# Dynamic convolution, layer norm and feed-forward: the first softmax in two pieces, the last tiles one by one, and a new order of the work at the start

## The chip, the cores and the metric

The kernel runs on one core of one Trainium2 chip. What counts is the time of one execution on the device in microseconds (us). Five engines work side by side, each through its own list of instructions in order: TensorE (PE; its weight loads are counted apart as PEld), VectorE (DVE), ScalarE (ACT), GpSimd (POOL) and SyncE (SP), which here issues transfers. Sixteen DMA engines carry the transfers.

## What is computed

`x` is (8, 4224, 192) and `weight_gen` (8, 4224, 8, 7), both float32. The reference, with the shapes put in, is:

```python
w = np.exp(w - np.max(w, axis=-1, keepdims=True))        # 8 heads, 7 taps for each token
w = w / (np.sum(w, axis=-1, keepdims=True) + 1e-09)
x_unf = x_pad[:, idx, :].reshape(B, S, 7, 8, 24)         # the token and the six before it
x = np.einsum('bshk,bskhg->bshg', w, x_unf).reshape(B, S, 192)
mu = np.mean(x, axis=-1, keepdims=True)
var = np.mean((x - mu) ** 2, axis=-1, keepdims=True)
xn = (x - mu) / np.sqrt(var + 1e-06) * g_ln
out = x + np.maximum(xn @ w_ch1, 0.0) @ w_ch2            # 192 -> 768 -> 192
```

The three parameters of the second half are float64.

## The kernel before

**Tiles.** The 33,792 tokens lie as 128 partitions by 264 tiles: a partition holds 264 neighbouring tokens, and a tile is one token of each partition, 192 values wide. The tiles go through in `PARTS` of 4, 4, 8 (five times), 12 (seventeen times), 8 and 4 tiles. The convolution works on chunks of 2 tiles (the first part), 4 tiles (the parts of 4 and 8) or 6 tiles (the parts of 12); the feed-forward works on groups of `NT` = 4 tiles. `SOFT` = (4, 8, 12, ...) says how many tiles one softmax covers.

**Softmax** (`softmax`, L449 to 487). After the load of the weights `w` come six steps, each for one softmax: the maximum over the taps (VectorE, L466), `sub` (GpSimd, L468), the exponential (ScalarE, L469), the sum (VectorE, L482), its logarithm (ScalarE, L484) and `less` (GpSimd, L486), which leaves the logarithm of the weights in `e`. A last exponential (`expw`, ScalarE, L498) is made for each chunk and puts its weights into PSUM (`wn`). For the chunks below `PMUL` = 3 there is one more (`keep`, L502), which puts them into `e` for GpSimd.

**Convolution** (`conv`, L492 to 577). A chunk has four multiplications by x, all L535: `c0`, `c1` and `c3` are two taps each and write one of five `pr` buffers, `c2` is one tap and writes `y`. VectorE runs them with the weights in `wn`, except `c3` of the chunks below `PMUL`, which GpSimd runs with the weights in `e`. In the first three chunks TensorE adds the seven products up (L560). In all later ones GpSimd does: two transfers that add one half of a `pr` buffer to the other (`d0`, `d1`, L541) and four additions to `y` (`a0` to `a3`, L538). So VectorE needs a free `pr` buffer for each multiplication of two taps, and GpSimd frees it.

**Norm** (`norm`, L598 on). For parts that begin below tile `STATS` = 8, VectorE takes mean and variance with `bn_stats`, two tiles at a time (L628). For the others ScalarE makes a sum (L611) and a sum of squares (L616) of each tile. Then come the root (ScalarE), a Newton step (VectorE) and the scaled tile `xh` (ScalarE, L686). The first two groups are turned on TensorE (L710), the others split into high and low fp16 halves and turned by a transfer (L756 to 762).

**Feed-forward.** The weights arrive as float64 words; VectorE makes float32 of them (L955, L964), then their power of two (`w_scale`, L982 to 988), from which ScalarE and TensorE make fp16 halves. For each group TensorE makes three `unit` products into `ph` (L780); each is evicted by ScalarE (`relu`, L796) and VectorE (`hlo`, the low half, L798). Two products (`p0`, `p1`, L832) bring the result into `po`, and VectorE merges it into `y` (L884), which is stored (L892). For the last group `output` (L861) does this for two tiles at a time, with one merge and one store for each pair.

**What sets the order.** Every operation has a name and a tile, and the table `PLACE` gives its place in one global order. Each engine runs its own operations in that order, so an operation waits for all that its engine has ahead of it. At the start, SyncE issues the weights of the first softmax (`w`, 4 tiles), those of the second (8 tiles), and then the first chunk's x in three transfers: `h0` (four tiles of the tokens ahead), `h` (the other two and the two tiles of the chunk) and `f` (the chunk's tiles in the partitions that begin a batch). The first multiplication (`c0`) needs `h0` alone, the second (`c1`) needs `h` too. Ahead of all of it ScalarE loads its table (L368) and makes a negated identity (`minus`, L380).

## Time and profile before

| | us |
|---|---|
| median of 3 runs (lowest, highest) | 844.35 (843.34, 845.62) |
| the profiled execution's own time | 843.82 |
| its span in the trace | 842.0 |
| busy: PE, DVE, ACT, POOL | 821.4, 736.5, 683.8, 701.6 |
| mean granted TensorE clock, as a share of full speed | 0.994 |

The span is the time from the first to the last instruction that the trace has; the 1.8 us around it belong to the execution but show no instruction. Busy times are sums over the whole span: TensorE is busy for 98% of it and the others for 81% to 87%. Since the start, the middle and the end of the program have different limits, the shares of the whole say little, and the rows below are read by stretch.

### The profile page before, as it was taken

To read this page: it belongs to the slowest core of one execution; us is meant where nothing else is said; L and a number is where in the kernel's file an instruction comes from. 1 tells how busy PE (TensorE), PEld (TensorE's weight loads), DVE (VectorE), ACT (ScalarE), POOL (GpSimd) and SP (SyncE) were. 2 spreads that over 40 slices of the span, in tenths; PEclk is the share of its full clock that TensorE was granted. 3 is DMA by queue.
4 is the path that set the end of the run, shared out by engine and by line. 5 is a ranking of instruction groups with operands and counts; after the bars stand their busy time and mean duration, and the time that the engine had idled before them with its cause. 6 is when DMAs were issued, how large, how long until landed. Compare 5 with 4: busy or idle time off the path is not lost.

```text
span 842.0 us, 37407 instructions
## 1 busy us (share of the span) xinstructions
PE 821.4 (98%) x16724; PEld 811.3 (96%) x16724; DVE 736.5 (87%) x685; ACT 683.8 (81%) x1774; POOL 701.6 (83%) x402
## 2 busy tenths in 40 slices
PE   6889999999999999999999999999999999999997
PEld 5669999999999999999999999999999999999997
DVE  7999999999999999999999999999989896745332
ACT  3899998898998899898888979988888878776431
POOL 4999999999999999999999999899798879624000
PEclk9889999999999999999999999999999999999999
DMA  9997997989999997889878997777877766352432
GB/s 228 206 211 153 221 162 170 204 160 205 193 195 191 199 215 167 178 186 215 190 153 202 188 217 174 164 185 163 180 153 162 165 145 129 78 116 68 80 65 58
DMA packets 133887, 140.88 MB, mean 167 GB/s; under 512 B 104294, under 2 KB 106222, under 8 KB 133726
## 3 DMA queue, kind: packets, MB, share of 16 engines
q1 hardware_dynamic: 120190, 88.16, 45.9%
q0 software_dynamic: 13536, 50.34, 30.8%
q8 instruction: 130, 2.13, 1.0%
q14 instruction: 31, 0.25, 0.1%
HBM read 36.43 MB, written 25.95 MB: 74 GB/s over the span
## 4 chain that ended last, share of the span: by engine, by line
PE 82%; DVE 11%; issue 2%; POOL 2%; ACT 1%; DMA 1%; SPq 1%; DVEq 0%; POOLq 0%; ACTq 0%
PE po L832 41%; PE ph L780 40%; DVE pr L535 6%; DVE hlo L798 2%; DVE y L535 1%; POOL y L538 1%; DMA x<-in_x_dram 1%; PE ph L861 1%; DVE y L884 1%; POOL pr L541 1%; ACT hh L796 0%; DVE mx L466 0%; ACT junk L611 0%; DVE sm L482 0%; DVE s L628 0%
## 5 line engine op out<-in xcount | busy, mean ns | idle before, releaser
L538 POOL TENSOR_TENSOR y<-y,pr 128x1152 f32<-128x1152 f32 (+1 forms) x188 | 488.3, 2625 | 13.0 <-DVE y L535 4.3
L780 PE MATMUL ph<-xT,c_w 64*128 64x256 f16 x7128 | 412.9, 269 | 1.9 <-DVE hlo L798 1.3
L780 PEld LDWEIGHTS <-c_w 64*128 64x128 f16 x7128 | 386.2, 94 | 3.1 <-issue 2.9
L832 PE MATMUL po<-c_w2h,hh 64*128 64x192 f16 x3120 | 388.0, 243 | 1.1 <-DVE y L884 1.1
L832 PE MATMUL po<-c_w2l,hh 64*128 64x192 f16 x3120 | 388.0, 243 | 0.0
L832 PE MATMUL po<-c_w2h,hlo 64*128 64x192 f16 x3120 | 388.0, 243 | 0.0
L535 DVE TENSOR_TENSOR pr<-x,wn 128x2304 f32<-128x2304 f32 (+2 forms) x147 | 333.2, 2276 | 4.3 <-POOL y L538 2.5
L832 PEld LDWEIGHTS <-hh 64*128 64x128 f16 x6240 | 309.7, 94 | 1.4 <-issue 1.3
L798 DVE SCALAR_TENSOR_TENSOR hlo<-ph,hh 128x1024 f16<-128x1024 f32 x198 | 239.4, 1217 | 73.1 <-ACT hh L796 72.6
L796 ACT ACTIVATE hh<-ph 128x1024 f16<-128x1024 f32 x198 | 200.2, 1014 | 84.8 <-PE ph L780 80.6
L832 PEld LDWEIGHTS <-hlo 64*128 64x128 f16 x3120 | 177.6, 94 | 0.0
L758 POOL TENSOR_TENSOR hl<-xh,hl 128x768 f16<-128x768 f32 x64 | 114.7, 1828 | 49.1 <-ACT hl L756 48.3
L686 ACT ACTIVATE xh<-y,s 128x192 f32<-128x192 f32 x264 | 125.8, 536 | 17.2 <-DVE s L674 12.1
L616 ACT ACTIVATE junk<-y,s 128x192 f32<-128x192 f32 x256 | 115.8, 452 | 7.9 <-PE po L832 1.8
L541 POOL DMA_DIRECT2D pr<-pr x94 | 93.2, 1054 | 26.6 <-DVE pr L535 22.1
L611 ACT ACTIVATE junk<-y 128x192 f32<-128x192 f32 x256 | 92.1, 360 | 12.5 <-PE po L832 4.1
L884 DVE SCALAR_TENSOR_TENSOR y<-po,c_fs,y 128x768 f32<-128x768 f32 (+1 forms) x83 | 67.9, 835 | 7.4 <-PE po L832 7.2
L535 DVE TENSOR_TENSOR y<-x,wn 128x1152 f32<-128x1152 f32 (+2 forms) x50 | 59.9, 1199 | 0.0
L756 ACT ACTIVATE hl<-xh 128x768 f16<-128x768 f32 x64 | 53.4, 836 | 1.6 <-PE po L832 0.7
L611 ACT ACTIVATION_READ_ACCUMULATOR junk<-y 128x1 f32 x256 | 48.1, 188 | 0.0
L616 ACT ACTIVATION_READ_ACCUMULATOR junk<-y,s 128x1 f32 x256 | 47.9, 187 | 0.0
L486 POOL TENSOR_TENSOR e<-e,sm 128x672 f32<-128x672 f32 (+2 forms) x23 | 37.8, 1645 | 6.6 <-ACT sm L484 6.6
(86 smaller groups left out, 308.3 us busy)
## 6 DMA issues: line engine op xcount, KB each, us to landing
pr<-pr POOLq DMA_DIRECT2D x68, 576.0 KB, 6.1
x<-in_x_dram SPq DMA_DIRECT2D x34, 576.0 KB, 6.0
...
pr<-pr POOLq DMA_DIRECT2D x26, 384.0 KB, 5.0
...
x<-in_x_dram SPq DMA_DIRECT2D x14, 384.0 KB, 6.2
out_dram<-y SPq DMA_DIRECT2D x13, 384.0 KB, 5.2
...
```

Source lines behind the costliest of these rows:

```text
L535: E.tensor_tensor(out=ov, in0=xv, in1=wv, op=ALU.mult)
L538: Q.tensor_tensor(out=flat(0), in0=flat(0), in1=flat(k), op=ALU.add)
L541: return Q.dma_start(flat(to), flat(k), accum_op=ALU.add, max_dma_last_dim=CHUNK * D * 4)
L611: A.activation(junk, at(y)[:, j, :], AF.Identity, scale=-SQ / D, accum_out=at(s4)[:, 3, t : t + 1])
L616: A.activation(junk, at(y)[:, j, :], AF.Square, scale=SQ, bias=at(s4)[:, 3, t : t + 1], accum_out=at(s4)[:, 0, t : t + 1])
L686: A.activation(paired(xh, t), at(y)[:, i, :].rearrange("p (c q) -> p c q", q=P // 2), AF.Identity, bias=row(2 if quick else 3)[:, g + t : ...
L758: lambda xh=xh, hl=hl: Q.tensor_tensor(out=halves(hl, True), in0=pairs(xh), in1=halves(hl, False), op=ALU.subtract),
L780: T_.matmul(ph[:, r, v * 2 * P : (v + 1) * 2 * P], W["w1"][rows, WB[r][c], w, f : f + P], xv[rows, a, c, :, :], start=(v == 0 and k == 0), ...
L796: lambda: A.activation(at(hh)[:, us, :], at(ph), AF.Relu), [ph], [(hh, u)])
L798: lambda: V.scalar_tensor_tensor(out=at(hlo)[:, us, :], in0=at(ph), scalar=0.0, in1=at(hh)[:, us, :], op0=ALU.max, op1=ALU.subtract),
L832: made.append(T_.matmul(at(po)[:, z, e * D : (e + 1) * D], token(b, 2 * z + e, j)[rows], W[w][rows, j, :], start=(ph == 0 and e == 0 and k ...
L884: V.scalar_tensor_tensor(out=ysl, in0=at(po)[:, zs[0] : zs[-1] + 1, : 2 * D], scalar=W["fs"][:, 0:1], in1=ysl, op0=ALU.mult, op1=ALU.add)
```

## The change

- The first softmax of 4 tiles becomes two of 2 tiles (`SOFT`), with pools of their own (`w0`, `e0`). One transfer brings the weights of both. In the first piece (`SUBV`, `LESSV`) both subtractions are VectorE's; in the second they stay GpSimd's.
- ScalarE, not SyncE, issues the second transfer of the first x (`h`). Its table load and `minus`, which stood ahead of everything, become operations with places of their own.
- GpSimd gets `c1` of the second chunk (`PTWO`) and `c3` of the fourth (`PMUL` 3 to 4), with the extra copies of the weights (`keep`) that they need.
- `STATS` = (4,) names the parts with `bn_stats`: the first part (tiles 0 to 3) now has ScalarE's sums and squares, the second still has `bn_stats`.
- `last` takes the place of `output`: the last four tiles go one by one, each with its own half of a PSUM buffer and a merge of 192 elements, with stores of two tiles, one and one.
- `PLACE` is a new table up to about place 495; from there on it is the old one, moved by about 11.

The diff, without all but two lines of the table:

```diff
 PARTS = (4,) * 2 + (8,) * 5 + (12,) * 17 + (8, 4)
-SOFT = (4, 8) + (12,) * 21
+SOFT = (2, 2, 8) + (12,) * 21
-PMUL = 3
-STATS = 8
+PMUL = 4
+STATS = (4,)
+PTWO = (2,)
+SUBV = (0,)
+LESSV = (0,)
...
-    'wload': (0, 1, 15, 26, 98, 102, 176, 495, 321, 482, 657, 761, 837, 1034, 613, 1145, 1282, 1182, 951, 1438,
+    'wload': (0, 3, 13, 46, 85, 190, 243, 505, 428, 102, 668, 772, 848, 1045, 624, 1156, 1293, 1193, 962, 1449,
...
+    pool("w0", 1, [P, 2 * FIRST, HK], F32)
+    pool("e0", 2, [P, FIRST * H, K], F32)
...
-    A.preload_act_table_set("natural_log_exp_and_others")
...
-    A.activation(minus, ident, AF.Copy, scale=-1.0)
...
-            sp(want, lambda: first(cut, PAD + n - cut), [], [("x", "h"), *cols], dma_ns((PAD + n - cut) * D * 4), "load")
+            op("ACT", 620, want, lambda: first(cut, PAD + n - cut, A), w=[("x", "h"), *cols],
+               dma=dma_ns((PAD + n - cut) * D * 4), kind="load")
+            op("ACT", 1300, ("table", 0), lambda: A.preload_act_table_set("natural_log_exp_and_others"), w=["table"])
+            op("ACT", 310, ("minus", 0), lambda: A.activation(minus, ident, AF.Copy, scale=-1.0), ["table"], ["minus"])
...
-        wb = pa["w"] = Buf("w")
-        sp(("wload", t0), lambda: SY.dma_start(at(wb)[:, :n, :].rearrange("p t f -> p (t f)"), tokens(wf, t0, n)), [], [wb],
+        if t0 == FIRST:
+            pa["w"] = softs[0]["w"]
+            return
+        wb = pa["w"] = Buf("w" if t0 else "w0")
+        n = n if t0 else 2 * FIRST
+        sp(("wload", t0), lambda: SY.dma_start(at(wb)[:, :n, :].rearrange("p t f -> p (t f)"), tokens(wf, t0, n)), [], [wb] if t0 else [(wb, 0), (wb, FIRST)],
...
-        step("Pool", 100 + 1.82 * m * K, "sub",
-             lambda: Q.tensor_tensor(out=at(e)[:, :m], in0=a3(wb), in1=wide(mx), op=ALU.subtract), [wb, mx], [e])
+        E, name, ns = (V, "V", v_ns(m * K)) if S0 in SUBV else (Q, "Pool", 100 + 1.82 * m * K)
+        step(name, ns, "sub",
+             lambda E=E: E.tensor_tensor(out=at(e)[:, :m], in0=a3(wb), in1=wide(mx), op=ALU.subtract), [wk, mx], [e])
...
-            if c < PMUL and i == 3:
+            if c < PMUL and (i == 3 or i == 1 and t0 in PTWO):
...
-        quick = S0 < STATS
+        quick = S0 in STATS
...
+    def last(gp, t, s):
+        e = t % 2
+        if e == 0:
+            gp["po"] = Buf("ph")
+        po, ks = gp["po"], triples(gp)
+        def mm():
+            for k, (b, j, w) in enumerate(ks):
+                T_.matmul(at(po)[:, e, :D], token(b, t, j), W[w][:, j, :], start=k == 0, stop=k == len(ks) - 1)
+        op("PE", 1490, ("o", s), mm, whole(gp), [(po, e), "pe"], lat=360.0)
+        y, j = ycol(gp["pa"], gp["g"] + t)
+        def final():
+            V.scalar_tensor_tensor(out=at(y)[:, j, :], in0=at(po)[:, e, :D], scalar=W["fs"][:, 0:1],
+                                   in1=at(y)[:, j, :], op0=ALU.mult, op1=ALU.add)
+        op("V", v_ns(D, 63), ("f", s), final, [(po, e), "fs"], [(y, j)])
+        if t > 0:
+            i, n = (j, 1) if t > 1 else (j - 1, 2)
+            t0 = chunks[-1]["S"] + i
+            sp(("u", s), lambda: SY.dma_start(tokens(out, t0, n), at(y)[:, i : i + n, :].rearrange("p t d -> p (t d)")),
+               [(y, i + q) for q in range(n)], [], dma_ns(n * D * 2))
...
     for t in range(NT):
-        output(prev, t, C)
+        last(prev, t, C)
```

The table moves instructions on every engine; three places show it. In the rows below a name's last number is the program's own count, and the number before it is the buffer.

First, VectorE at the start, before: maxima and sums of the first and second softmax (L466, L482), and the first multiplications (L535).

```order
L466 TENSOR_REDUCE mx0_92<-w0_64 128x32
L482 TENSOR_REDUCE sm0_94<-w0_64 128x32
L466 TENSOR_REDUCE mx1_93<-w1_65 128x64
L535 TENSOR_TENSOR pr0_76<-x_63,wn0_102 128x2x384
L535 TENSOR_TENSOR y0_67<-x_63,wn0_102 128x384
L482 TENSOR_REDUCE sm1_95<-w1_65 128x64
L535 TENSOR_TENSOR pr1_77<-x_63,wn0_102 128x2x384
L535 TENSOR_TENSOR pr2_78<-x_63,wn1_103 128x2x384
L535 TENSOR_TENSOR pr4_80<-x_63,wn1_103 128x2x384
```

The same place in the changed kernel (L481 maximum, L484 `sub`, L498 sum, L503 `less`, L552 multiplication; `w00` is the pair of pieces, `e01` the first piece):

```order
L481 TENSOR_REDUCE mx0_95<-w00_67 128x16
L481 TENSOR_REDUCE mx1_96<-w00_67 128x16
L484 TENSOR_TENSOR e01_69<-w00_67,mx1_96 128x112
L498 TENSOR_REDUCE sm0_97<-w00_67 128x16
L503 TENSOR_TENSOR e01_69<-e01_69,sm0_97 128x112
L552 TENSOR_TENSOR pr0_79<-x_63,wn0_105 128x2x384
L498 TENSOR_REDUCE sm1_98<-w00_67 128x16
L552 TENSOR_TENSOR y0_70<-x_63,wn0_105 128x384
L481 TENSOR_REDUCE mx0_95<-w0_64 128x64
L552 TENSOR_TENSOR pr1_80<-x_63,wn0_105 128x2x384
L498 TENSOR_REDUCE sm0_97<-w0_64 128x64
```

The first piece now passes through VectorE alone but for ScalarE's steps, the sum of the second piece stands behind the first multiplication, and the maximum and sum of the 8-tile softmax (`w0`) stand two and one multiplications further back than before.

Second, GpSimd at the start, before: the subtractions of the first three softmaxes (L468, L486), its `c3` of the first three chunks (L535) and the first additions by transfer (L541).

```order
L468 TENSOR_TENSOR e0_96<-w0_64,mx0_92 128x224
L486 TENSOR_TENSOR e0_96<-e0_96,sm0_94 128x224
L468 TENSOR_TENSOR e1_97<-w1_65,mx1_93 128x448
L486 TENSOR_TENSOR e1_97<-e1_97,sm1_95 128x448
L535 TENSOR_TENSOR pr3_79<-x_63,e0_96 128x2x384 x2
L468 TENSOR_TENSOR e0_96<-w2_66,mx0_92 128x672
L535 TENSOR_TENSOR pr4_80<-x_63,e1_97 128x2x768
L541 DMA pr3_79<-pr3_79 128x768
L541 DMA pr2_78<-pr2_78 128x768
```

In the changed kernel (L484, L503 subtractions, L552 multiplications, L555 additions, L558 additions by transfer):

```order
L484 TENSOR_TENSOR e00_68<-w00_67,mx0_95 128x112
L503 TENSOR_TENSOR e00_68<-e00_68,sm1_98 128x112
L484 TENSOR_TENSOR e0_99<-w0_64,mx0_95 128x448
L552 TENSOR_TENSOR pr2_81<-x_63,e01_69 128x2x384
L503 TENSOR_TENSOR e0_99<-e0_99,sm0_97 128x448
L552 TENSOR_TENSOR pr4_83<-x_63,e00_68 128x2x384
L552 TENSOR_TENSOR pr1_80<-x_63,e00_68 128x2x384
L484 TENSOR_TENSOR e1_100<-w1_65,mx1_96 128x672
L552 TENSOR_TENSOR pr2_81<-x_63,e0_99 128x2x768
L555 TENSOR_TENSOR y3_73<-y3_73,pr2_81 128x768
L558 DMA pr3_82<-pr3_82 128x768
```

GpSimd has lost the two subtractions of the first piece and has two more multiplications, `pr1_80` (`c1` of the second chunk) and the second `pr2_81` from `e0_99` (`c3` of the fourth); its first additions to `y3` now stand among them.

Third, VectorE at its fifth chunk, before: `c0` (`pr4_80`), the power of two of the first weights (L982 to 988), `c3` (`pr3_79`), `c1` (`pr2_78`), and `bn_stats` of the second part (L628) behind all of it.

```order
L535 TENSOR_TENSOR pr4_80<-x_63,wn0_102 128x2x768
L982 TENSOR_SCALAR c_r1_125<-po0_106 128x1
L983 TENSOR_SCALAR c_r1_125<-c_r1_125 128x1
L985 TENSOR_SCALAR c_r1_125<-c_r1_125 128x1
L986 RECIPROCAL c_r1_125<-c_r1_125 128x1
L988 TENSOR_SCALAR c_gi_122<-c_g_121,c_r1_125 128x1 x2
L535 TENSOR_TENSOR pr3_79<-x_63,wn0_102 128x2x768
L535 TENSOR_TENSOR pr2_78<-x_63,wn0_102 128x2x768
L955 SCALAR_TENSOR_TENSOR po0_106<-pr1_77,po0_106 128x384
L964 SCALAR_TENSOR_TENSOR hlo1_91<-x_63,po0_106 128x384
L628 BN_STATS s42_100<-y2_69 128x6 x2
```

In the changed kernel (L552 multiplications, L1023 to 1029 power of two, L645 `bn_stats`):

```order
L552 TENSOR_TENSOR pr0_79<-x_63,wn1_106 128x2x768
L552 TENSOR_TENSOR y4_74<-x_63,wn1_106 128x768
L1023 TENSOR_SCALAR c_r1_126<-po0_109 128x1
L1024 TENSOR_SCALAR c_r1_126<-c_r1_126 128x1
L1026 TENSOR_SCALAR c_r1_126<-c_r1_126 128x1
L1027 RECIPROCAL c_r1_126<-c_r1_126 128x1
L1029 TENSOR_SCALAR c_gi_123<-c_g_122,c_r1_126 128x1 x2
L552 TENSOR_TENSOR pr2_81<-x_63,wn1_106 128x2x768
L645 BN_STATS s41_102<-y2_72 128x6 x2
L552 TENSOR_TENSOR pr3_82<-x_63,wn1_106 128x2x768
```

`c1` (`pr2_81`) and both `bn_stats` now stand ahead of `c3` (`pr3_82`), which stood right behind the power of two.

## Rows read from the trace of the kernel before

**Rows 1.** Busy time by stretch: window, length, engines (instructions), PEclk, DMA share, GB/s.

```profile
0.00:8.00 8.00, 0.00 (x0) 0.00 (x0) 2.19 (x8) 3.44 (x7) 3.76 (x10) 1.00 0.65 166
8.00:20.00 12.00, 11.60 (x58) 11.50 (x59) 11.97 (x16) 4.03 (x11) 5.48 (x5) 1.00 1.06 267
20.00:52.70 32.70, 27.35 (x108) 18.90 (x107) 31.68 (x50) 28.02 (x78) 31.54 (x22) 0.84 0.93 217
52.70:100.00 47.30, 46.30 (x950) 45.81 (x951) 46.96 (x48) 45.55 (x125) 46.61 (x31) 1.00 0.85 184
100.00:148.60 48.60, 47.22 (x1000) 46.77 (x995) 47.06 (x44) 41.31 (x109) 47.37 (x31) 1.00 0.87 174
148.60:800.00 651.40, 651.38 (x13868) 651.22 (x13869) 582.49 (x511) 551.61 (x1437) 565.24 (x306) 1.00 0.79 168
```

**Rows 2.** Timeline of TensorE: the first product (start, duration, instruction, wait before).

```profile
52.72 4.19 PE L780 MATMUL ph<-xT,c_w 64*128 64x256 f16 x72 [0.58 <-ACT c_w2l L1080]
```

**Rows 3.** Who TensorE waited for, 52.6 to 842 us: total, number, longest.

```profile
PE ph L780 <- DVE hlo L798: 1.3, 3, 0.7
PE po L832 <- DVE y L884: 1.1, 1, 1.1
```

**Rows 4.** Chain of waits, 117 to 150 us: start, time, instruction.

```profile
123.47 1.86 POOL y L538
```

**Rows 5.** Who GpSimd waited for, 0 to 48 us: total, number, longest.

```profile
POOL e L486 <- ACT sm L484: 3.9, 2, 2.6
```

**Rows 6.** Timeline, 0 to 9 us: VectorE, GpSimd and ScalarE.

```profile
3.31 0.39 DVE L466 TENSOR_REDUCE mx<-w 128x32 f32<-128x224 f32 x1 [2.28 <-DMA w<-in_weight_gen_dram]
3.78 0.57 POOL L468 TENSOR_TENSOR e<-w,mx 128x224 f32<-128x224 f32 x1 [1.48 <-DVE mx L466]
6.22 0.97 POOL L468 TENSOR_TENSOR e<-w,mx 128x448 f32<-128x448 f32 x1
6.30 0.27 ACT L498 ACTIVATE wn<-e 128x112 f32<-128x112 f32 x1 [0.75 <-POOL e L486]
7.30 0.95 DVE L535 TENSOR_TENSOR pr<-x,wn 128x768 f32<-128x768 f32 x1 [1.58 <-DMA x<-in_x_dram]
```

**Rows 7.** VectorE's groups by form: busy, mean ns of one, idle before.

```profile
L535 DVE TENSOR_TENSOR pr<-x,wn 128x1536 f32<-128x1536 f32 x41 | 70.9, 1744 | 0.1
L884 DVE SCALAR_TENSOR_TENSOR y<-po,c_fs,y 128x768 f32<-128x768 f32 x47 | 47.4, 1009 | 4.4 <-PE po L832 4.3
L535 DVE TENSOR_TENSOR pr<-x,wn 128x768 f32<-128x768 f32 x4 | 3.6, 947 | 1.6 <-DMA x<-in_x_dram 1.6
L628 DVE BATCH_NORM_STATS2 s<-y 128x6 f32<-128x384 f32 x4 | 2.2, 560 | 0.0
L884 DVE SCALAR_TENSOR_TENSOR y<-ph,c_fs,y 128x384 f32<-128x384 f32 x2 | 1.2, 618 | 4.4 <-PE ph L861 4.4
```

**Rows 8.** DMA issues, 0 to 6 us: KB each, median us from issue to landing.

```profile
x<-in_x_dram SPq DMA_DIRECT2D x2, 360.0 KB, 5.3
```

**Rows 9.** GpSimd's multiplications by form.

```profile
L535 POOL TENSOR_TENSOR pr<-x,e 128x768 f32<-128x768 f32 x2 | 3.1, 1547 | 3.2 <-PE ph L560 3.2
L535 POOL TENSOR_TENSOR pr<-x,e 128x1536 f32<-128x1536 f32 x1 | 2.9, 2904 | 1.2 <-ACT e L502 1.2
```

**Rows 10.** ScalarE's sums and squares, from the costliest groups of the page.

```profile
L616 ACT ACTIVATE junk<-y,s 128x192 f32<-128x192 f32 x256 | 115.8, 452 | 7.9 <-PE po L832 1.8
L611 ACT ACTIVATE junk<-y 128x192 f32<-128x192 f32 x256 | 92.1, 360 | 12.5 <-PE po L832 4.1
```

**Rows 11.** Timeline, 20 to 40 us: VectorE and GpSimd.

```profile
34.66 3.42 DVE L535 TENSOR_TENSOR pr<-x,wn 128x1536 f32<-128x1536 f32 x2
36.50 1.81 POOL L538 TENSOR_TENSOR y<-y,pr 128x768 f32<-128x768 f32 x1 [0.41 <-DVE pr L535]
```

**Rows 12.** DMA issues, 800 to 842 us: the stores.

```profile
out_dram<-y SPq DMA_DIRECT2D x2, 384.0 KB, 3.4
out_dram<-y SPq DMA_DIRECT2D x2, 192.0 KB, 2.5
```

More of the change, by code (lines that the diff above doesn't have):

```diff
@@ new lines @@
+    'table': (1,),
+    'minus': (4,),
+    'w_load': (38, 22, 20,),
+    'w_gain': (59, 35, 53,),
+    'w_load2': (27,),
+    'w_as': (103,),
+    'w_ap': (105,),
+    'w_av': (112, 115,),
+    'w_an': (120,),
+    'w_cs': (65,),
+    'w_cp': (64,),
+    'w_cv': (68, 72,),
+    'w_cn': (111,),
+    'w_s1': (124, 128,),
+    'w_d': (135, 132,),
+    'w_h': (148, 133,),
+    'w_l': (165, 136,),
+    'w_lc': (177, 140,),
+    'w_m': (182, 180, 157, 145,),
+    'w_c2s': (84, 98, 121,),
+    'w_c2p': (86, 95, 146,),
@@ new lines @@
+    'exp': (12, 21, 37, 73, 126, 223, 381, 490, 603, 648, 720, 806, 914, 1034, 1116, 1159, 1287, 1423, 1470,
+        1592, 1656, 1834, 1860, 2034,),
+    'sum': (14, 25, 40, 239, 384, 502, 612, 656, 732, 845, 957, 1043, 1149, 1189, 1290, 1446, 1522, 1616, 1687,
+        1846, 1871, 2045,),
+    'log': (15, 29, 42, 101, 164, 275, 417, 511, 615, 669, 776, 869, 980, 1047, 1171, 1262, 1353, 1469, 1535,
+        1619, 1710, 1867, 1880, 2071,),
+    'less': (17, 31, 44, 110, 181, 310, 431, 519, 617, 702, 781, 893, 996, 1069, 1204, 1267, 1355, 1489, 1570,
+        1661, 1752, 1870, 1947, 2103,),
```

122 lines of the change are left out of this document (49 added, 73 removed), and 239 rows, old and new, of the table PLACE.

## The prediction

> **What bounds the kernel now.** The first view is the table of busy time by stretch [rows 1]. From 148.6 us to 800 us TensorE is busy for 651.38 of 651.40 us, and the diff leaves the order of that part as it was (the table's entries from there on are the old ones, moved by about eleven). So a change can move the end only in two places: in the time at which TensorE comes out of the stretch before 148.6 us, and after its last product. In the stretch before, three engines are full at once. VectorE is busy for 46.96 and 47.06 us of the two windows of 47.3 and 48.6 us, GpSimd for 46.61 and 47.37, and ScalarE for 45.55 in the first. TensorE starts its first product at 52.72 us [rows 2], and from then to 148.6 us it waits 2.4 us in all, each time for VectorE: 1.3 us in three waits for a low half (hlo) and 1.1 us in one for a merge of finished rows into y (L884) [rows 3]. That last wait ends the stretch. The chain of waits [rows 4] shows what stands behind it: the merge is simply next in VectorE's order, and further back VectorE had got its buffer from GpSimd's addition at 123.47. VectorE's multiplications write five pr buffers, and GpSimd's additions free them, so VectorE can't run ahead of GpSimd by more than those.
>
> The same table tells where there is room. GpSimd idles 4.24 us up to 8 us and 6.52 us from 8 to 20 us, then 1.16, 0.69 and 1.23 us: 13.84 us before 148.6. VectorE from 8 us on idles 0.03, 1.02, 0.34 and 1.54 us. So at the start VectorE is the full one and GpSimd the empty one; most of GpSimd's early waits are for ScalarE's logarithm [rows 5].
>
> **The change part by part.** I make the sum against the profiled execution's own 843.82 us, which lies 0.53 us under the median of the three runs; the result is then put onto the median.
>
> *First softmax.* Before, the weights' arrival lets the maximum start at 3.31, GpSimd subtracts at 3.78, and ScalarE has the first weights in PSUM by 6.57; the first multiplication still waits for x until 7.30 [rows 6]. In the change the piece that is needed first goes over 112 elements and stays on VectorE. Its seven steps were 224 elements wide; GpSimd's subtraction costs 0.57 us for 224 and 0.97 for 448 [rows 6], so 0.37 for 112. VectorE's multiplication of 768 takes 0.947 us and of 1536 takes 1.744 [rows 7], 1.04 ns an element over 0.15 us, so 0.27 for 112. Two maxima, a subtraction, a sum and a subtraction of 0.27 and three ScalarE steps of 0.27 with a small gap before each [rows 6] make 2.3 us: weights ready at 5.6 instead of 6.57. The gate is then x. Its two loads take 5.3 us from issue to landing [rows 8]; the first is now issued one transfer earlier and doesn't queue behind the 224 KB of the second softmax. If only the issue moves, it lands at about 6.6; if the bytes ahead are also gone, before 5.6. I take 6.0, so VectorE starts 1.3 us earlier. ScalarE's own load goes out behind its table and its negated identity, in idle time; SP's list gets shorter by one issue.
>
> By the Trainium skill's page "SBUF — State Buffer", section "Who interferes with whom", a VectorE instruction with two SBUF inputs and a GpSimd instruction that reads SBUF shut each other out for a whole instruction. No run here shows it; the two new VectorE subtractions have both inputs in SBUF and run while GpSimd subtracts the other piece. By that rule the weights would be ready up to 0.37 us later, at 6.0, and the sum would be the same.
>
> *VectorE to GpSimd.* c1 of the second chunk (768 elements) and c3 of the fourth (1536) leave VectorE: 0.95 + 1.74 us there, 1.55 + 2.90 us on GpSimd [rows 7, 9]. The two bn_stats of the first part, 0.56 us each [rows 7], go to ScalarE as four sums of 0.36 us and four sums of squares of 0.45 [rows 10], 3.2 us and the reading of each sum, where [rows 1] show 4.56, 7.97 and 4.68 us idle in the three windows up to 52.7. VectorE is thus relieved of 3.8 us and starts 1.3 us earlier; the sum of the second piece comes behind the first multiplication, and waits for the second softmax's exponential and for the fourth chunk's weights give back about 2 us. VectorE would be 2.2 us early when it works out the weights' power of two.
>
> *GpSimd.* It gets 4.45 us and loses two halves of a subtraction, 0.40 us: 4.05 us more to do before 148.6. That is free only as far as it fills the 13.84 us. I followed its list. Up to 8 us it idles 5.5 us, more than now, since it waits for the second piece's logarithm, which stands behind VectorE's first multiplication. From the second softmax's subtraction at 8.15 on, the inputs of each next operation are there: 0.5 us idle up to 20 us instead of 6.52. Then comes one new wait. In the order shown for VectorE, the fourth multiplication of the fifth chunk now stands behind the second (pr2 ahead of pr3) and behind both bn_stats, and GpSimd starts that chunk's DMA addition before its plain ones. Now VectorE runs those two from 34.66 to 38.08 and GpSimd waits 0.41 us for the first [rows 11]. In the change VectorE has the first at 34.0 while GpSimd is there at 32.8, and the second, the one that it waited for before, at 36.7 instead of 36.4, just when GpSimd wants it. So 1.8 us from 20 to 52.7 us, and about 0.9 us of small gaps after. Sum 8.7 us; 5.1 us are filled, 4.05 us of it with the added work. GpSimd, and with it the release of TensorE, comes 1.1 us earlier (I use 1.2 with rounding). VectorE's own lead is larger and is held by the pr buffers. TensorE's own bound is further off: I find its first product some 2.4 us earlier, and 2.4 us of its waits can go. Bounds: idle of 6.6 us (x at 5.6, no wait at 32.8) gives -3.2; no idle filled at all gives +4.05.
>
> *Tail.* The last merge works on one tile: 618 ns for 384 elements and 1009 for 768 [rows 7], so 0.42 for 192, 0.2 less. The last store is 96 KB: 384 KB land in 3.4 us and 192 KB in 2.5 [rows 12], so by the slope 0.45 less, and nothing if the fixed part is all. I take -0.5 for both (bounds -0.2 and -0.65). TensorE's last 72 products are the same.
>
> Sum: -1.2 - 0.5 = -1.7 us: 842.1 on the profiled execution, **842.6 us** on the median.
>
> **Rivals.** (a) *x doesn't come earlier.* The first table shows the 16 DMA engines full from 8 us on, and 65% busy before [rows 1]. Then the first multiplication stays at about 7.2, everything on GpSimd shifts with it, and only the tail is left: 844.35 - 0.5 = 843.9. By the Trainium skill's page "DMA: Bandwidth & Descriptors", section "Issuing engines are not separate DMA queues", a transfer started from another engine runs on the same 16 DMA engines and saves only the issuing time; the row on their share agrees with the premise, and this rival is what follows. Against it: the first load of x also moves ahead of 224 KB, and that is not a matter of who issues it. (b) *VectorE's lead passes through.* If GpSimd finds no wait at 32.8 and the gaps of 0.69 and 1.23 us close, its idle is 6.7 us: -3.1 - 0.5 gives 840.8; TensorE's own bound (-4.8) would allow 839.1. For it: each wait of TensorE is for VectorE. Against: the pr buffers. (c) *GpSimd is overfull, slower than before.* Its two new multiplications need copies of the weights from ScalarE, and the fourth chunk's also a load of x that is due at about the time GpSimd gets there. If they leave GpSimd idle as it is now, up to 13.2 us, the 4.05 us add to the path: +3.4 - 0.5 gives 847.2. It decides from an idle of 9.8 us on (13.84 - 4.05); above that the stretch gets longer.
>
> **How the numbers follow.** Forecast 0.40, (a) 0.21, (b) 0.28, (c) 0.11. A measurement of this kernel can tell about 0.3% from no change, 2.5 us: faster means under 841.8, slower over 846.9. Faster is nearly all of (b) and a sixth of the forecast, 0.34; slower is most of (c), 0.09; within is the rest, 0.57. The range reaches from 839.1 (all of (b), down to TensorE's own bound) to 845.2 (all of (a), a mild (c)). The forecast's own range is 841.2 to 843.9.
>
> **What would show it.** The first multiplication on VectorE at 6.0 (5.6 to 6.6 right, 7.2 for (a)); GpSimd's idle from 8 to 20 us near 0.5, and up to 148 us near 8.7 (6.7 for (b), over 9.8 for (c)); a wait of GpSimd for VectorE's pr near 33 us; the first product near 50.3; the last wait of TensorE for L884 ending at 147.4 instead of 148.6; from the last matmul to the end 0.5 us less. The forecast is wrong in its frame if TensorE waits after 150 us, or if its clock is at its lower level when the products begin.

## The result, and the profile after

The changed kernel takes 851.80 us (median of 6 runs, 850.72 to 853.91); in the same comparison the kernel before takes 844.39 us. The ratio is 1.0091, with a 95% interval of 1.0075 to 1.0108: 7.4 us slower, where 1.7 us faster was forecast, and above the forecast's range of 839.1 to 845.2. The profiled execution takes 853.91 us, the longest of the six, with a span of 852.1.

The first view is the chain of waits of the changed kernel, from its first 30 us (start, time, what). It answers to [rows 4] and [rows 8], which had no such stretch:

```profile
...
2.57 4.72 DMA w<-in_weight_gen_dram
7.29 0.02 issue
7.31 10.06 DMA x<-in_x_dram
17.36 0.02 issue
17.39 0.96 DVE pr L552
```

The chain runs through two transfers. The weights of the 8-tile softmax are issued at 2.57 and land at 7.29; 0.02 us later ScalarE's transfer of x (`h`) begins, takes 10.06 us, and only then, at 17.39, VectorE goes on with its second multiplication. The timeline of ScalarE, VectorE, GpSimd and the issues of transfers (ACTq, SPq) at that place (start, time, instruction, idle before and what ended it) answers to [rows 6]:

```profile
0.74 1.28 ACT L441 ACT_TABLE_LOAD   x1 [0.74 <-PEq L1170]
2.33 0.31 ACT L442 ACTIVATE minus<-ident 128x128 f16<-128x128 f32 x1 [0.30 <-POOL ident L381]
...
3.70 0.38 POOL L484 TENSOR_TENSOR e<-w,mx 128x112 f32<-128x112 f32 x1 [1.40 <-DVE mx L481]
...
3.83 0.38 DVE L484 TENSOR_TENSOR e<-w,mx 128x112 f32<-128x112 f32 x1
...
7.31 1.49 ACTq L434 DMA_DIRECT2D x<-in_x_dram  x1
...
8.90 0.30 ACT L485 ACTIVATE w<-e 128x112 f32<-128x112 f32 x1 [6.27 <-issue]
...
9.88 0.28 DVE L503 TENSOR_TENSOR e<-e,sm 128x112 f32<-128x112 f32 x1 [0.37 <-ACT sm L500]
...
10.55 0.95 DVE L552 TENSOR_TENSOR pr<-x,wn 128x768 f32<-128x768 f32 x1 [0.40 <-ACT wn L515]
...
17.38 2.68 SPq L451 DMA_DIRECT2D x<-in_x_dram  x2
17.39 0.95 DVE L552 TENSOR_TENSOR pr<-x,wn 128x768 f32<-128x768 f32 x1 [4.71 <-DMA x<-in_x_dram]
```

The kernel before has these two lines there, the first exponential and the multiplications from the second on:

```profile
4.38 0.39 ACT L469 ACTIVATE w<-e 128x224 f32<-128x224 f32 x1 [1.75 <-POOL e L468]
...
9.16 2.67 DVE L535 TENSOR_TENSOR pr<-x,wn 128x768 f32<-128x768 f32 x3
```

ScalarE had loaded its table and made its negated identity by 2.64, and was then free. Yet its issue (ACTq) begins at 7.31, and the first exponential, which stands behind it on ScalarE, at 8.90 instead of 4.38 before. So the first multiplication starts at 10.55 instead of 7.30, and the second, which needs `h`, at 17.39 instead of 9.16. SyncE is held up as well: after an issue at 14.84 its next one, a load of x, comes only at 17.38, just after `h` has landed.

Busy time by stretch answers to [rows 1] (window, length, PE, PEld, DVE, ACT, POOL with their counts, clock, DMA share, GB/s):

```profile
0.00:8.00 8.00, 0.00 (x0) 0.00 (x0) 1.02 (x7) 1.59 (x2) 2.06 (x8) 1.00 0.66 157
8.00:20.00 12.00, 5.22 (x17) 4.96 (x18) 5.28 (x10) 3.04 (x10) 3.49 (x4) 0.92 1.05 276
20.00:52.70 32.70, 30.02 (x139) 23.52 (x138) 30.74 (x49) 29.01 (x83) 30.57 (x21) 0.93 0.72 165
52.70:100.00 47.30, 42.91 (x822) 40.05 (x823) 46.45 (x49) 44.58 (x120) 46.99 (x32) 1.00 0.77 169
100.00:148.60 48.60, 46.41 (x980) 45.68 (x976) 46.09 (x44) 40.44 (x106) 45.91 (x31) 1.00 0.93 183
```

GpSimd idles 5.94, 8.51, 2.13, 0.31 and 2.69 us: 19.58 us up to 148.6, against 13.84 before. TensorE's first product starts at 58.93 instead of 52.72 [rows 2], and its last one ends at 847.59 instead of 837.51, 10.1 us later. What TensorE waits for from 52 to 200 us (total, number, longest) answers to [rows 3]:

```profile
PE ph L797 <- DVE hlo L815: 3.7, 7, 0.9
...
PE po L849 <- DVE y L925: 0.7, 1, 0.7
PE po L849 <- ACTq L859: 0.4, 1, 0.4
```

The waits for VectorE's low halves have grown from 1.3 to 3.7 us. Of the two signs that the prediction's frame is wrong, one is there: TensorE waits after 150 us, 0.9 us for a low half and 0.4 us for ScalarE's sequencer, in a stretch that is some 10 us late here. The other is not: the clock column of the table above has 1.00 from 52.7 us on. At the other end nothing was won. The last merges of the changed kernel, in VectorE's timeline from 844.6 us on, answer to [rows 7]:

```profile
844.74 0.74 DVE L884 SCALAR_TENSOR_TENSOR y<-ph,c_fs,y 128x192 f32<-128x192 f32 x2 [2.13 <-PE ph L878]
847.63 0.74 DVE L884 SCALAR_TENSOR_TENSOR y<-ph,c_fs,y 128x192 f32<-128x192 f32 x2 [2.15 <-PE ph L878]
```

Its last stores, among the DMA issues from 810 us on (KB each, us to landing), answer to [rows 12]:

```profile
out_dram<-y SPq DMA_DIRECT2D x1, 192.0 KB, 2.5
out_dram<-y SPq DMA_DIRECT2D x2, 96.0 KB, 2.1
```

The two merges of a pair start together, after the pair's second product, and the last two stores, of 96 KB each, are issued one behind the other, at 848.07 and 848.70. From the last product's end to the end of the span there are 4.54 us; before the change there were 4.51.

### The profile page after: what moved, and what is told of

Same layout as the page of the kernel before. It is cut to its first block, busy times and chain, and to the rows that moved or that the text cites. A ratio compares the mean times of both kernels' runs of the same rounds, so it can differ in the third digit from the quotient of the medians.

```text
span 852.1 us, 37438 instructions
## 1 busy us (share of the span) xinstructions
PE 822.2 (96%) x16724; PEld 775.1 (91%) x16724; DVE 734.7 (86%) x687; ACT 687.7 (81%) x1793; POOL 705.2 (83%) x404
## 3 DMA queue, kind: packets, MB, share of 16 engines
q8 instruction: 130, 2.13, 1.0%
## 4 chain that ended last, share of the span: by engine, by line
PE 78%; POOL 12%; DMA 3%; DVE 2%; issue 2%; ACT 2%; SPq 0%; DVEq 0%; POOLq 0%; ACTq 0%
PE po L849 39%; PE ph L797 38%; POOL y L555 8%; POOL pr L558 2%; POOL hl L775 2%; DVE pr L552 1%; DMA xT<-hl 1%; DMA x<-in_x_dram 1%; PE ph L577 1%; PE ph L878 1%; DMA w<-in_weight_gen_dram 1%; ACT junk L633 1%; ACT junk L628 0%; POOL e L484 0%; POOL e L503 0%
## 5 line engine op out<-in xcount | busy, mean ns | idle before, releaser
L555 POOL TENSOR_TENSOR y<-y,pr 128x1152 f32<-128x1152 f32 (+1 forms) x188 | 490.6, 2641 | 11.1 <-DVE y L552 4.3
L797 PEld LDWEIGHTS <-c_w 64*128 64x128 f16 x7128 | 351.3, 94 | 38.8 <-issue 5.8
L552 DVE TENSOR_TENSOR pr<-x,wn 128x2304 f32<-128x2304 f32 (+2 forms) x145 | 331.2, 2292 | 9.9 <-DMA x<-in_x_dram 4.7
L849 PEld LDWEIGHTS <-hh 64*128 64x128 f16 x6240 | 286.3, 94 | 4.5 <-issue 1.2
L849 PEld LDWEIGHTS <-hlo 64*128 64x128 f16 x3120 | 155.6, 94 | 0.3 <-issue 0.3
L633 ACT ACTIVATE junk<-y,s 128x192 f32<-128x192 f32 x260 | 117.6, 452 | 7.8 <-PE po L849 1.5
L558 POOL DMA_DIRECT2D pr<-pr x94 | 93.0, 1057 | 31.8 <-DVE pr L552 23.7
L628 ACT ACTIVATE junk<-y 128x192 f32<-128x192 f32 x260 | 93.5, 360 | 15.5 <-POOL y L555 5.5
L552 DVE TENSOR_TENSOR y<-x,wn 128x1152 f32<-128x1152 f32 (+2 forms) x50 | 60.1, 1202 | 0.1
L628 ACT ACTIVATION_READ_ACCUMULATOR junk<-y 128x1 f32 x260 | 48.8, 188 | 0.0
L503 POOL TENSOR_TENSOR e<-e,sm 128x672 f32<-128x672 f32 (+2 forms) x23 | 36.4, 1584 | 11.2 <-ACT sm L500 11.2
```

Source lines behind the costliest of these rows:

```text
L552: E.tensor_tensor(out=ov, in0=xv, in1=wv, op=ALU.mult)
L555: Q.tensor_tensor(out=flat(0), in0=flat(0), in1=flat(k), op=ALU.add)
L558: return Q.dma_start(flat(to), flat(k), accum_op=ALU.add, max_dma_last_dim=CHUNK * D * 4)
L628: A.activation(junk, at(y)[:, j, :], AF.Identity, scale=-SQ / D, accum_out=at(s4)[:, 3, t : t + 1])
L633: A.activation(junk, at(y)[:, j, :], AF.Square, scale=SQ, bias=at(s4)[:, 3, t : t + 1], accum_out=at(s4)[:, 0, t : t + 1])
L797: T_.matmul(ph[:, r, v * 2 * P : (v + 1) * 2 * P], W["w1"][rows, WB[r][c], w, f : f + P], xv[rows, a, c, :, :], start=(v == 0 and k == 0), ...
```

## The experiments

Four kernels with one part undone or done alone, then eight that follow what was left. In each, "the last product" is the end of TensorE's last product in the profiled execution (before: 837.51).

**1. SyncE issues `h` again.** All else is the changed kernel's.

```diff
-            op("ACT", 620, want, lambda: first(cut, PAD + n - cut, A), w=[("x", "h"), *cols],
-               dma=dma_ns((PAD + n - cut) * D * 4), kind="load")
+            sp(want, lambda: first(cut, PAD + n - cut), [], [("x", "h"), *cols], dma_ns((PAD + n - cut) * D * 4), "load")
```

> The changed kernel with one edit undone: SyncE issues the second transfer of the first x (h) again, in its old place in the table; all else is the changed kernel's. Theory (the wait of ScalarE): in the trace after the change ScalarE's issue of h stands from 2.64 to 7.31 us, until the 8-tile weights land at 7.29, and the exponential of the first softmax stands behind it (8.90); h lands at 17.37, and the second multiplication starts at 17.39. Without that wait h is issued near 3.2 and lands near 8.7, the first multiplication starts at 6.5 and the second no later than 9; the time is the forecast of the prediction, 842.6 (841 to 844.5). Rival 1 (the added work on GpSimd and the new order cost the 7 us): the second multiplication comes early all the same, and the time stays above 848. Rival 2 (the 16 DMA engines are full, x is late whoever issues it): the second multiplication still starts after 13 us, and the time stays above 848.

845.77 us, ratio to before 1.0021 (1.0011 to 1.0032). The last product ends at 839.70. `h` lands at 8.60. VectorE's first and second multiplication in the timeline of this run:

```profile
6.22 0.95 DVE L551 TENSOR_TENSOR pr<-x,wn 128x768 f32<-128x768 f32 x1 [0.78 <-DMA x<-in_x_dram]
...
8.63 0.95 DVE L551 TENSOR_TENSOR pr<-x,wn 128x768 f32<-128x768 f32 x1 [0.28 <-DMA x<-in_x_dram]
```

TensorE's first product in it:

```profile
51.18 4.10 PE L796 MATMUL ph<-xT,c_w 64*128 64x256 f16 x72
```

Both rivals fall: most of the 7.4 us was ScalarE's issue. It is 6.0 us from median to median, and 5.1 if each run is set against the kernel before in its own comparison (843.49 here). But the time isn't the forecast's either: it is 2 us over the kernel before, not 1.7 under.

**2. ScalarE issues `h`, but first of all.** The places of the load and of the table load change; nothing else.

```diff
-    'load': (2, 5, 6, 9, ...
-    'table': (1,),
+    'load': (2, 1, 6, 9, ...
+    'table': (1.5,),
```

> The changed kernel, but ScalarE issues h as its first instruction, ahead of its table load and the negated identity; all else is the same. Theory (the wait of ScalarE, not ScalarE as issuer): the issue starts before 1 us, waits for nothing, and h lands by 7 to 8 us; the table load and the negated identity come 0.7 to 1.5 us later, in idle time. The time is that of the run with SyncE's issue or up to 1 us under it: 841 to 844. Rival (an issue from ScalarE costs ScalarE itself, or shares the DMA engines badly): the first exponential still starts after 7 us or h lands after 12, and the time stays above 847.

844.93 us, ratio 1.0023 (1.0013 to 1.0032); the last product ends at 838.42. `h` lands at 5.17. The issue and the first exponential in the timeline of this run:

```profile
0.74 1.48 ACTq L434 DMA_DIRECT2D x<-in_x_dram  x1
...
4.25 0.30 ACT L485 ACTIVATE w<-e 128x112 f32<-128x112 f32 x1 [0.40 <-DVE e L484]
```

So it isn't ScalarE as issuer; it is what this issue waits for at its later place. The program as built says what that is. The first row is ScalarE's issue in the changed kernel, the second the one in this run:

```
L434 DMA x<-in_x_dram 120x1x768 [waits DMAHW2_49]
L434 DMA x<-in_x_dram 120x1x768
```

The loads, transposes and stores that SyncE and ScalarE issue in this program signal their completion on eight counters, DMAHW0 to 7, which they take in turn, and a transfer is not issued until the one that had its counter before has landed. In the changed kernel ScalarE's load is the eleventh to take one and gets the third, which is that of the 8-tile weights; issued first, it finds its counter free. The trace of the changed kernel agrees: the issue at 7.31 waits on the counter that the 8-tile weights raise at 7.29, and SyncE's issue at 17.38 waits on the same one, which `h` raises at 17.36. Why it takes its turn only as the eleventh, though the table places it ahead of `f`, which takes the fourth counter, isn't shown. The trace of the kernel before shows the same rule on SyncE: its issues at 11.50, 14.02 and 14.98 follow landings of the transfers eight places ahead at 11.49, 14.00 and 14.96.

**3. The kernel before, with ScalarE's issue of `h` alone**, behind the table load and the negated identity.

```diff
-            sp(want, lambda: first(cut, PAD + n - cut), [], [("x", "h"), *cols], dma_ns((PAD + n - cut) * D * 4), "load")
+            op("ACT", 620, want, lambda: first(cut, PAD + n - cut, A), w=[("x", "h"), *cols],
+               dma=dma_ns((PAD + n - cut) * D * 4), kind="load")
```

> The kernel before with this one part of the change alone: ScalarE issues h, behind its table load and its negated identity; nothing else is changed. Theory (the wait of ScalarE): ScalarE's issue waits for the landing of an earlier transfer (here h0, near 6 to 7 us), the exponential of the first softmax stands behind it and starts after 7 instead of at 4.4; h lands at 15 to 17 instead of 8.74, and the second multiplication waits for it. Slower than before by 4 to 10 us: 848 to 854. Rival 1 (the loss is the new order and GpSimd's added work): 844 to 846, as before.

853.18 us, ratio 1.0114 (1.0100 to 1.0128). This edit alone makes the kernel before slower than the whole change does. Its timeline shows the same picture; here the third counter is that of `h0`, which lands at 6.86:

```profile
6.88 1.49 ACTq L428 DMA_DIRECT2D x<-in_x_dram  x1
...
8.48 0.39 ACT L470 ACTIVATE w<-e 128x224 f32<-128x224 f32 x1 [5.84 <-issue]
...
16.55 2.68 DVE L536 TENSOR_TENSOR pr<-x,wn 128x768 f32<-128x768 f32 x3 [3.91 <-DMA x<-in_x_dram]
```

**4. The changed start, SyncE's issue, the last tiles in pairs again.** As experiment 1, with `output` in the place of `last` and its old places.

```diff
-        last(prev, t, C)
+        output(prev, t, C)
```

> As the run in which SyncE issues h, and besides the last four tiles go in pairs again, as before the change; the start is the same. The tail of the prediction: one by one is worth 0.5 us (0.2 to 0.65), so this is 0.5 slower than that run. Rival (in the trace after the change the merges of the last two tiles both start after the last product, 847.63 and 847.96, and two stores are issued one behind the other; from the last product to the end are 4.53 us, before 4.51): no difference, within 0.2 us.

845.64 us, ratio 1.0015 (1.0005 to 1.0025), against 845.77 for experiment 1; from the last product to the end 4.51 us, against 4.54. The last tiles one by one are worth nothing as they were written: the rival stands.

**5. ScalarE issues `h0` first**, and SyncE `h` in the place of `h0`.

```diff
+            sp(want, lambda: first(cut, PAD + n - cut), [], [("x", "h"), *cols], dma_ns((PAD + n - cut) * D * 4), "load")
+            op("ACT", 620, want, lambda: first(0, cut, A), w=[("x", "h0")], dma=dma_ns(cut * D * 4), kind="load")
```

> The changed kernel, but ScalarE issues h0 (which the first multiplication needs) as its first instruction, and SyncE issues h in h0's old place. Sum that the runs so far give: the end moves by GpSimd's added work (4.05 us) and its idle up to 148.6 us less the 13.84 of before; measured 12.37 with SyncE's issue (sum +2.6, end +2.2) and 10.67 with ScalarE's first (sum +0.9, end +0.9). Theory (GpSimd's idle is what counts): h0 lands by 5.5, the first multiplication starts at 5.9 instead of 7.04, GpSimd's idle up to 8 us falls from 5.9 to 4.9; the end comes 0.5 to 1.2 us earlier than with h first: last product near 837.5. Rival (VectorE's buffers or the transposes hold GpSimd later anyway): the idle comes back after 20 us, and the end is as with h first.

843.93 us, ratio 1.0007 (0.9997 to 1.0016): as before the change, and 1.0 us under experiment 2, which is what the theory had (0.5 to 1.2). The first multiplication starts at 5.76 and GpSimd idles 5.55 us up to 8 us, 0.4 less than with `h` first (the forecast here was 1.0 less). The profiled execution took 845.71 us and its last product ended at 839.42, not at 837.5. The times of this kernel fall into two groups, 843.2 to 844.5 and 845.7 to 846.0, and so do those of experiments 1, 2 and 4. Of these four kernels only experiment 2 has its profile (844.71) from its lower group. In GpSimd's waits the three others have a row that it lacks, the second one here, in this run (18 to 152 us):

```profile
POOL pr L557 <- DVE pr L551: 2.4, 3, 1.4
POOL pr L557 <- DMA xT<-hl: 2.0, 1, 2.0
```

GpSimd's transfers that add (L557) and the transposes are kept apart in this program, and the new order puts two of those additions behind two transposes; near 139 us GpSimd waits there for 2.0 us. That this wait makes the two groups is argued from four profiles, not shown.

**6 and 7. GpSimd's two added multiplications go back to VectorE**, once on the kernel of experiment 2 and once on that of experiment 5.

```diff
-PMUL = 4
-PTWO = (2,)
+PMUL = 3
+PTWO = ()
-    'keep': (19, 43, 52, 55,),
+    'keep': (19, 43, 52,),
```

> The changed kernel with ScalarE's issue of h first, and besides GpSimd's two added multiplications (c1 of the second chunk, c3 of the fourth) are VectorE's again, in their places of the table. Theory (GpSimd's sum, 4.45 us of added work against 13.84 us of idle): GpSimd has 0.40 us less to do than before instead of 4.05 more; if its idle stays at 10.7 us the end comes 3.5 us earlier than before; VectorE takes 2.69 us more where it idles 6.9 us up to 148.6, so some of GpSimd's idle grows: 840 to 842 us, 1.5 to 4 under the run with h first. Rival (VectorE is the full engine, as the prediction had it): GpSimd then waits for VectorE's multiplications, its idle grows by the 2.7 us and more, and the time is that of the run with h first or above it, 844 to 846.

> Both edits: ScalarE issues h0 first, and the two added multiplications are VectorE's again. Theory: the gains add, first multiplication at 5.9 and GpSimd without the added 4.45 us: 839 to 841.5, under the kernel before by 2 to 4. Rival (VectorE full): 843.5 to 846, no gain over ScalarE's issue of h0 alone.

845.92 us, ratio 1.0027 (1.0016 to 1.0037), and 846.68 us, ratio 1.0028 (1.0016 to 1.0039). No gain, rather a loss: the theory falls, VectorE is the full engine at this place. GpSimd's waits in the first of the two, 18 to 152 us (its profiled execution took 848.22 us, 2.3 over its median):

```profile
POOL y L555 <- DVE y L552: 4.3, 1, 4.3
POOL pr L558 <- DMA xT<-hl: 3.0, 2, 2.0
POOL pr L558 <- DVE pr L552: 2.7, 2, 1.3
```

Its first plain addition waits 4.3 us for VectorE. What it no longer multiplies, it idles: 5.31 us from 8 to 20 us instead of 1.14. So, in this order, the added work on GpSimd was not what cost the time.

**8. Each merge placed ahead of the next tile's products**, on the kernel of experiment 2.

```diff
-    'f': (... 2402, 2405, 2407, 2410, 2412,),
+    'f': (... 2402, 2403.5, 2405, 2408.5, 2412,),
```

> The changed kernel with ScalarE's issue of h first, and besides each of the last four merges is placed ahead of the next tile's products in the table (it was behind them). In the kernel as changed TensorE signals once for two tiles (after 36 products), so both merges start after the second. Theory: TensorE now signals after each tile's 18, the merge of the third tile starts 1.5 us before the last product's end, its store is out before the last one, and from the last product to the end are 4.0 to 4.2 us instead of 4.53. Rival (the last store's landing alone sets it): 4.4 to 4.6, no difference.

847.89 us, ratio 1.0050 (1.0034 to 1.0065). From the last product to the end there are now 3.88 us instead of 4.51, a little less than the theory's 4.0 to 4.2. But the two tiles of a pair share a PSUM buffer, and TensorE now waits for each merge before it goes on. TensorE's waits from 150 us on in this run:

```profile
PE ph L878 <- DVE y L884: 1.1, 2, 0.6
PE ph L797 <- DVE hlo L815: 0.8, 1, 0.8
```

0.63 us won behind the last product, 1.1 lost ahead of it. The rest of this run's time is at the start, where its profile has 3.0 us of waits for transposes; why all four of its runs lie in the upper group isn't explained by the edit, and stays open.

**9. Two additions ahead of the transposes**, on the kernel of experiment 5: GpSimd's `d0` and `d1` of the fourteenth chunk get the places that they had, in relation to the transposes, before the change.

```diff
-    'd0': (... 435, 486,
+    'd0': (... 435, 458.5,
-    'd1': (... 444, 489,
+    'd1': (... 444, 466.2,
-    'lo': (... 412, 464, 468,
+    'lo': (... 412, 466.4, 468,
```

> The run in which ScalarE issues h0 first, with one edit in the table: GpSimd's two additions by transfer of the fourteenth chunk (d0, d1) stand ahead of its two subtractions for the transposes again, as they did before the change; they stood 4 to 6 places behind. No other engine's order changes. So far GpSimd waits near 139 to 141 us for the transposes in all profiles but one (1.6 to 2.4 us), and the times of one kernel fall in two groups about 2 us apart (with h0 first: 843.2 to 844.5 and 845.7 to 846.0). Theory (that wait is the rest of what the forecast missed): GpSimd waits for no transpose, its idle from 100 to 148.6 us falls from 3.14 to 1.2, only the lower group is left, and the time is 842.3 to 843.8. Rival 1 (VectorE has the chunk's products 2.6 us later than before, so GpSimd waits for them instead): GpSimd waits 1 us and more for pr near 130, the time stays at 843.5 to 846. Rival 2 (the transposes, now behind the additions, come too late for TensorE): a wait of TensorE for xT near 147, 844 to 846.

846.83 us, ratio 1.0037 (1.0023 to 1.0052). The theory falls here: the wait for the transposes is gone, and another took its place. GpSimd's waits for VectorE's products, 18 to 200 us:

```profile
POOL pr L557 <- DVE pr L551: 4.5, 5, 1.4
```

TensorE's waits from 40 us on:

```profile
PE ph L796 <- DVE hlo L814: 3.7, 7, 0.8
PE po L848 <- DVE y L924: 2.0, 2, 1.2
```

GpSimd now waits 4.5 us for VectorE's products in place of 2.4, and the transposes, some 5 us later than in experiments 1 and 2, seem to hold up what comes behind them: TensorE's waits for merges rise from 0.8 in experiment 5 to 2.0 us. Rival 1 is in the trace, with 1.1 us near 130 us. Rival 2's own sign, a wait of TensorE for the transposed tiles, is not; what stands near there is a wait of VectorE, 3.03 us up to 146.67, for ScalarE's eviction of a product, and that the late transposes are behind it is argued. In the new order VectorE has this chunk's products about 2 us later than before the change (c0 ready at 129.7 to 130.5 instead of 127.9), so the additions cannot simply go back to their old place.

**10. The same with a PSUM buffer for each of the last tiles.**

```diff
-        e = t % 2
-        if e == 0:
-            gp["po"] = Buf("ph")
+        e = 0
+        gp["po"] = Buf("ph")
```

> As the run just above with the two additions moved ahead, and besides each of the last four tiles has a PSUM buffer of its own (TensorE then signals after each 18 products; the merges stand where the change put them). Theory: from the last product to the end 3.9 us as with the merges placed early (3.88), and without the 1.1 us for which TensorE waited there for the merges: 0.6 us under that run. Rival: TensorE waits for a merge to free a buffer, 0.3 to 1.1 us, and nothing is left.

846.50 us, ratio 1.0031 (1.0019 to 1.0043): 0.3 under experiment 9 where 0.6 was expected, and within the spread of both. The profile shows the difference: 3.88 us from the last product to the end, four merges that start one by one (836.81, 838.21, 839.70, 841.18), and no wait of TensorE for a merge there. The merges still stand behind the next tile's products, so a buffer for each tile is enough for a signal for each.

**11. The kernel before, ScalarE issuing `h0` first**, ahead of its table load and the negated identity.

```diff
-            sp(want, lambda: first(0, cut), [], [("x", "h0")], dma_ns(cut * D * 4), "load")
+            op("ACT", 620, want, lambda: first(0, cut, A), w=[("x", "h0")], dma=dma_ns(cut * D * 4), kind="load")
...
```

> The kernel before with one edit: ScalarE issues h0 as its first instruction, ahead of its table load; the order of everything else is the kernel before's. Theory (GpSimd's sum sets the end): h0 lands by 5.5 instead of 7.20, the first multiplication starts when its weights are there, 6.7 instead of 7.30, and GpSimd's idle falls by 0.5: 0.3 to 0.7 us under the kernel before (842.8 to 843.5 where before has 843.5 to 843.8). Rival 1 (h, which the second multiplication needs, sets it): no difference. Rival 2 (an issue from ScalarE costs in itself): slower than before by 1 us or more.

844.07 us, ratio 0.9999 (0.9990 to 1.0008). The first multiplication does start earlier, at 6.56, but the maximum of the second softmax, whose weights now land at 5.95 instead of 4.76, comes later; GpSimd's idle up to 148.6 us is 14.18 us, none won. Rival 1's outcome, by another path than it named.

**12. The kernel before, with the tail alone**: one by one, a PSUM buffer for each tile, and the merges in the order of the changed kernel, each behind the next tile's products.

```diff
-        output(prev, t, C)
+        last(prev, t, C)
-    'f': (... 2391, 2395, 2398,),
+    'f': (... 2391, 2393.5, 2394.5, 2397.5, 2398,),
...
```

> The kernel before with the tail alone: the last four tiles one by one, each with a PSUM buffer of its own and its merge placed so that TensorE signals after each 18 products; the start and the order of all else are the kernel before's. Theory (the tail's term of the prediction was lost to the signal for two tiles, not to the idea): the last product ends where it ends before (837.5), from there to the end 3.9 us instead of 4.51, and the time is 0.6 us under the kernel before: the only version here that is under it. Rival: TensorE waits for a merge (0.3 to 1.1 us) and nothing is left.

843.04 us where the kernel before has 843.91; ratio 0.9990 (0.9981 to 0.9999). Its last merges on VectorE:

```profile
833.81 0.42 DVE L866 SCALAR_TENSOR_TENSOR y<-ph,c_fs,y 128x192 f32<-128x192 f32 x1 [0.65 <-PE ph L860]
835.21 0.42 DVE L866 SCALAR_TENSOR_TENSOR y<-ph,c_fs,y 128x192 f32<-128x192 f32 x1 [0.99 <-PE ph L860]
836.70 0.42 DVE L866 SCALAR_TENSOR_TENSOR y<-ph,c_fs,y 128x192 f32<-128x192 f32 x1 [1.07 <-PE ph L860]
838.18 0.42 DVE L866 SCALAR_TENSOR_TENSOR y<-ph,c_fs,y 128x192 f32<-128x192 f32 x1 [1.07 <-PE ph L860]
```

A merge 1.5 us apart for each tile, and 3.89 us from the last product to the end instead of 4.51. But the last product of the profiled execution ends at 838.15, not at 837.5, so that its span is the 842.0 us of before; the gain stands in the medians alone. It is the one version here under the kernel before, by 0.1%, and its interval ends just below 1.

## Why the prediction was wrong

**The step that failed** stands in its part on the first softmax: "ScalarE's own load goes out behind its table and its negated identity, in idle time". It was costed at nothing. The issue waited from 2.64 to 7.31 us, the first exponential stood behind it, and `h` landed at 17.36 us; the prediction looked only at `h0`, for the first multiplication, and not at `h`, for the second. Undone alone, it brings back 5.1 to 6.0 us (experiment 1); done alone, it costs 9.7 (experiment 3). What stood in the place of idle time was a wait of 4.67 us for a counter, with all of ScalarE's work behind it. The eight counters could have been read from SyncE's issues in the trace before, and the wait from the built program.

**Rival (a)**, x not earlier, is not what happened. `h0` did come earlier, at 6.55 us instead of 7.20 (forecast 6.0); what came late was `h`, of which neither the forecast nor the rival speaks. The reason named there has a part in it: by the Trainium skill's page "DMA: Bandwidth & Descriptors", section "Issuing engines are not separate DMA queues", transfers of all issuers run on the same 16 engines. The trace agrees, since `h`, issued at 7.31 behind ten transfers of SyncE, took 10.06 us, against 5.4 when SyncE issued it at 3.21 in experiment 1. The wait before the issue is not in that rule.

**The sum by GpSimd's idle time held as a frame**, with a limit told below the table, and rival (c)'s condition (idle above 9.8 us makes it slower) is the one that came true, by another cause than the one it named. Idle is 148.6 us less GpSimd's busy time in the five windows; the sum is the work added to GpSimd (4.05 us in the changed order, -0.40 with its two multiplications back, 0 in the kernel before) plus the idle, less 13.84:

| kernel | idle, us | sum, us | last product, us later |
|---|---|---|---|
| changed | 19.58 | +9.8 | +10.1 |
| 1, SyncE issues h | 12.37 | +2.6 | +2.2 |
| 2, ScalarE issues h first | 10.67 | +0.9 | +0.9 |
| 4, 1 with pairs | 12.14 | +2.4 | +2.1 |
| 5, ScalarE issues h0 first | 11.99 | +2.2 | +1.9 |
| 6, 2 without the added work | 18.54 | +4.3 | +4.4 |
| 7, 5 without the added work | 17.87 | +3.6 | +3.5 |
| 3, before, ScalarE's issue | 21.43 | +7.6 | +7.8 |
| 11, before, h0 first | 14.18 | +0.3 | +0.5 |
| 12, before, tail | 14.52 | +0.7 | +0.6 |
| 9, 5 with additions ahead | 11.19 | +1.4 | +2.9 |
| 10, 9 with a buffer for each tile | 11.40 | +1.6 | +3.6 |
| 8, 2 with early merges | 12.76 | +3.0 | +4.0 |

All rows are of the profiled executions. The sum holds within 0.4 us in ten of the thirteen kernels. In experiment 8 the difference is the 1.1 us of waits for merges at the end. In experiments 9 and 10 it is 1.5 and 2.0 us short: the stretch isn't over at 148.6 us there, and GpSimd idles another 1.7 and 1.9 us more than before between 148.6 and 300 us. Counted to 300 us, with the 1.1 us in experiment 8, the sum holds within 0.5 us in all thirteen.

**The size of the idle** was the second error, and it is why even the kernels with a good issue don't reach the forecast's 8.7 us. The rows are those of experiment 2, which has the least idle:

```profile
0.00:8.00 8.00, 0.00 (x0) 0.00 (x0) 2.53 (x11) 2.94 (x7) 2.07 (x8) 1.00 0.72 192
8.00:20.00 12.00, 11.86 (x57) 11.79 (x58) 10.32 (x14) 6.94 (x22) 10.86 (x8) 1.00 1.05 302
20.00:52.70 32.70, 26.76 (x130) 18.18 (x130) 31.57 (x48) 30.75 (x90) 30.44 (x22) 0.95 0.88 201
52.70:100.00 47.30, 45.95 (x950) 45.05 (x946) 46.21 (x51) 44.66 (x120) 46.91 (x32) 1.00 0.74 163
100.00:148.60 48.60, 46.61 (x981) 45.89 (x977) 46.44 (x41) 40.83 (x111) 47.65 (x31) 1.00 0.95 196
```

Idle up to 8 us is 5.93 (forecast 5.5), then 1.14 (0.5), 2.26 (1.8), and 1.34 behind 52.7 us (0.9): 2.0 us more in small terms, which turns the -1.1 that the forecast's own terms give (it used -1.2) into +0.9. In experiments 1, 4 and 5 the idle is 3.3 to 3.7 us over the forecast, and 2.0 to 2.7 us of that are GpSimd's waits for the transposes; that wait was no term of the forecast. "About 0.9 us of small gaps after" had no row behind it; it took the later part as unchanged, though the table had changed the order of the additions up to 140 us.

**Right were**, in the kernels where the issue doesn't wait, the first multiplication (5.76 and 6.22 in experiments 5 and 1, forecast 6.0; but 7.04 in experiment 2, where `h0` lands at 6.91), the wait for pr with its cause (1.4 us near 35 us, forecast 1.2 near 33), the work moved to GpSimd (it fills idle time; back on VectorE it costs, experiments 6 and 7), and the first product (50.7 to 51.6 us in experiments 1, 2 and 5, forecast 50.3). VectorE's lead did pass to TensorE's start and was lost again by 130 us.

**The tail's term**, -0.5, came out as 0. Of its two parts the shorter merge was there (0.42 us in experiment 12, as worked out), and the smaller store (2.1 us from issue to landing, forecast 2.0). What was missed: both merges of a pair start only after the pair's 36 products, because the two tiles share a PSUM buffer and each merge stands behind the next tile's products. Both merges and both stores then come at the end, and the second store's issue, 0.63 us behind the first, takes back what the two parts give. Undoing either is enough: with early merges (experiment 8) or a buffer for each tile (10 and 12) 3.88 or 3.89 us remain behind the last product, a term of -0.6. Only the buffers do it without a wait of TensorE.

**The rule on VectorE and GpSimd.** The prediction weighed the Trainium skill's page "SBUF — State Buffer", section "Who interferes with whom". VectorE's two-input subtraction of 112 elements took 0.38 us at 3.83, while GpSimd subtracted from 3.70 to 4.08, and its second subtraction, of the same form, 0.28 us at 9.88, alone. The two overlap in the trace (which gives GpSimd's spans only roughly), and the difference is 0.10 us here, not a whole instruction of 0.37; the measurement decides. That sharing makes the 0.10 us isn't shown, since no run has the first subtraction alone.
